# Linear attention and a two-matrix block on one Trainium2 core: Down stage in pairs of token groups, seven block products for eight in half the features

## The chip, the cores and the metric

The kernel runs on one core of one Trainium2 chip. The metric is the device time of one execution in microseconds (us), as the median of several runs. Beside the runs there is one profiled execution, whose trace gives the span from the first to the last instruction and every instruction's start and duration.

## The reference

```python
B, H, S, D = 4, 8, 768, 64          # batch, heads, sequence, head size; block = 64
for b in range(S // block):         # chunked linear attention with a decay per head
    qb, kb, vb = q[:, :, sl], k[:, :, sl], v[:, :, sl]
    intra = (qb kb^T * Dmask) vb
    inter = (qb * lam_pow) kv_state
    out[:, :, sl] = intra + inter
    kv_state = lam_block * kv_state + (kb * rev_pow)^T vb
x = out.transpose(0, 2, 1, 3).reshape(3072, 512)
h = x @ w_in                        # 512 x 2048
g = np.maximum(0.01 * h, h)
return g @ w_out                    # 2048 x 512
```

The data are float32; the two matrices arrive as float64 and are turned into float32 on the chip. A product of float32 matrices is made of three matmuls on reduced-precision parts (called h, l and m in the code), which have to be made of every operand first.

## The kernel before

**Tiling.** There are 24 chunks of 128 tokens, and four chunks make a group of T = 512 tokens; so NG = 6 groups. The 2048 features are cut into NP = 8 blocks p of 256.

**Stages.** A round (`round_of`) is the attention of one chunk: matmuls in `quad` (L313), VectorE and GpSimd steps for decay masks and states (L419, L423, L452, L459, L462), and the parts of x into the tiles X[g % 2] (L507 to L510). `up(g, p)` multiplies one group with one block of w_in (L640): per half block h and l passes, an ACT scaling in the bank (L658), the m pass, and the leaky ReLU on ACT (L661) into one of two buffers gs; a DMA (L664) stores 128 x 1024 values in memory, as G[g][p]. `to_float32` and `parts` turn float64 blocks of w_in and w_out into parts (L566 to L602); w_out goes to memory (`WO`) and comes back (`w_out_parts`, L621) when the last group of Up is done with the block's place in W. In the Down stage `down_load(g, p)` brings G[g][p] back (L675) into a ring of four slots and makes its parts: h on ACT (L682), l and m on VectorE (L683, L685). `down(g, p)` multiplies two blocks with w_out (L700): for each of four chunks of the group 12 matmuls, with the tokens as the stationary operand. Four pairs of banks hold the sums; after the eighth block ACT (L722) and VectorE (L729) combine a pair, and a DMA (L732) stores 128 x 512 results.

**Order.** Nothing is scheduled by the framework. Every step is handed to the class `Plan` with its engine, an assumed duration, and the names that it reads and writes. `Plan.emit` is a list scheduler: it gives each engine the step that can start first, ties by rank, and the program is issued in that order. A DMA's result is assumed 3.5 us after its end, and `slack` adds to that. Ranks come from the place in a list `seq`, which is written out by hand: rounds, `wi` (w_in), `up`, `wo`, `wp` (w_out's parts), `dl` and `dn`. All DMAs are issued on SyncE's queue (SP), in one order; an engine waits in its own order too, so a step that waits holds up what is behind it.

Of the kernel before, what the change touches and what calls it, by code (L numbers as in the profile page):

```python
# [8 lines left out]
F32 = mybir.dt.float32  # L9
F32R = mybir.dt.float32r  # L10
# [152 lines left out]
def kernel(  # L163
# [34 lines left out]

    DV = 10
# [21 lines left out]
    bank = {"b10": b1[0], "b11": b1[1], "b2": b2}  # L221
# [3 lines left out]
    raw = [sb([P, 2 * d_model], f"raw{i}") for i in range(NRAW)]  # L225
    lows = [sb([P, d_model], f"low{i}", I32) for i in range(2)]
    w32 = sb([P, 2, d_model], "w32")
    w32f = w32.rearrange("p h n -> p (h n)")
    tt = [raw[-1][:, i * T:(i + 1) * T] for i in range(2)]
    gs = [sb([P, 2, T], f"gs{i}") for i in range(2)]  # L230
    WO = [dram.tile([P, 2 * d_model], F32, name=f"wo{p}", tag=f"wo{p}") for p in range(NP)]
    G = [[dram.tile([P, 2 * T], F32, name=f"g{g}_{p}", tag=f"g{g}_{p}") for p in range(NP)] for g in range(NG)]
# [130 lines left out]
    def load_subs(c):  # L363
        b, n, i = of(c)
        count = run(c)[1]
        for nm, src, pieces in zip("kq", (k, q), subs(c, count)):
            for sub, lo, hi, keys in pieces:
                add("DVE", 0.0, lambda: None, [], keys)
                for y in range(lo, hi):
                    for a in range(4):  # L370
                        h = y // 2 + (2 * y + a // 2) % HP * 2
                        z = src[b, h, n * C:(n + count) * C, a % 2 * C4:(a % 2 + 1) * C4]
                        o = sub[a * C4:(a + 1) * C4, y - lo, :]
                        move(0.55, lambda o=o, z=z: nc.sync.dma_start(
                                out=o.rearrange("j (m i) -> j m i", i=C4), in_=z.rearrange("(m j) i -> j m i", j=C4)),
                            keys, [f"{nm}s{y}{a}"], issue=SUBL, rank=RUNS.get(c, (4.0, 0.4))[0] + RUNS.get(c, (4.0, 0.4))[1] * (4 * y + a))
# [179 lines left out]
    def to_float32(kind, p, h, dst, key, after=()):  # L556
# [20 lines left out]
        move(1.6, get, after, [f"raw{j}"])  # L577
# [9 lines left out]
    def parts(p, src, keys):  # L587
# [10 lines left out]
        difference(p)  # L598
# [12 lines left out]
    NR = 4  # L611
    graw = [att[:, j * 2 * T:(j + 1) * 2 * T] for j in range(NR)]

# [5 lines left out]
    def w_out_parts(p):  # L619
        j = p % NR  # L620
        add("DMA", 1.5, lambda: nc.sync.dma_start(out=graw[j], in_=WO[p]), [f"WO{p}"], [f"gr{j}"], rank=-3.0)  # L621
        parts(p, graw[j], [f"gr{j}"])


    n_t = n_g = 0
    n_b = -EARLY

    def up(g, p, lo=0, hi=GC):
# [20 lines left out]
        for fs in blocks:  # L649
# [9 lines left out]
            for i, f in enumerate(fs):  # L659
                add("PE", us, lambda f=f, d=b[:, i, :]: product(d, f, 2), keys("m"), [kb])  # L660
            add("ACT", ns, lambda b=b, r=r: nc.scalar.activation(out=r, in_=b, func=AF.Prelu, bias=0.0, scale=1.0 / WS, alpha=0.01),  # L661
                [kb], [f"gs{jg}"], rank=-1.5)
        move(1.5 * (hi - lo) / GC + 0.1,
            lambda: nc.sync.dma_start(out=G[g][p].rearrange("p (f t) -> p f t", f=2)[:, :, toks], in_=y), [f"gs{jg}"], [f"G{g}{p}"], slack=GSLACK)  # L664

    acc = [[z[:, i].rearrange("p y t -> p (y t)") for i in range(2)] for z in (psc, po)] + [
        [b1[0], b2], [b1[1], pt.rearrange("p y t -> p (y t)")]]
    ACC = [["psc", "psc"], ["po", "po"], ["b10", "b2"], ["b11", "pt"]]  # L670
    ring = [[X[j // 2][z].rearrange("p k t -> p (k t)")[:, j % 2 * 2 * T:(j % 2 + 1) * 2 * T] for z in range(3)] for j in range(NR)]

    def down_load(g, p):
        j = (g * NP + p) % NR
        add("DMA", 1.5, lambda: nc.sync.dma_start(out=graw[j], in_=G[g][p]), [f"G{g}{p}"], [f"gr{j}"])  # L675
        h, l, m = ring[j]
        reads = [f"gr{j}"]

        def wr(z):
            return [f"r{z}{j}"] + [f"x{z}{j // 2}{cc}" for cc in range(GC)] if g == 0 and p < NR else [f"r{z}{j}"]  # L680

        add("ACT", 1.05, lambda: nc.scalar.activation(out=h, in_=graw[j], func=AF.Copy, bias=0.0, scale=NEAR), reads, wr("h"))  # L682
        add("DVE", 1.25, lambda: nc.vector.scalar_tensor_tensor(l, graw[j], 1.0, h.bitcast(F32), op0=ALU.mult, op1=ALU.subtract),  # L683
            reads + [f"rh{j}"], wr("l"))
        add("DVE", 1.25, lambda: nc.vector.scalar_tensor_tensor(m, l.bitcast(F32), -S, h.bitcast(F32), op0=ALU.mult, op1=ALU.add),  # L685
            [f"rh{j}", f"rl{j}"], wr("m"))

    def down(g, p):

        nonlocal n_t  # L690
        for tb in range(GC):
            done = p + 2 == NP
            very_last = done and g == NG - 1 and tb == GC - 1

            def go(pps, zs, cols, tb=tb):
                for pp in pps:
                    j = (g * NP + pp) % NR
                    for f in range(2):
                        for z in zs:
                            nc.tensor.matmul(acc[tb][z // 2][:, cols], lhsT=ring[j][z][:, f * T + tb * P:f * T + (tb + 1) * P],  # L700
                                             rhs=W[pp][z][:, f * d_model:(f + 1) * d_model][:, cols],
                                             start=pp == 0 and f == 0 and z != 1, stop=pp == NP - 1 and f == 1,
                                             skip_group_check=True)

            def needs(pps, zs):
                return [f"{x}{z}{y}" for pp in pps for z in zs for x, y in (("r", (g * NP + pp) % NR), ("w", pp))]


            every = slice(0, d_model)
            halves = [slice(0, d_model // 2), slice(d_model // 2, d_model)]  # L710
            one, two = (p,), (p + 1,)
            order = [(one, (0, 1, 2), every), (two, (0, 1, 2), every)]
            if very_last:
                order = [(one + two, (0, 1), every)] + [(one + two, (2,), x) for x in halves]
            for pps, zs, cols in order:
                part_of = f"{halves.index(cols)}" if cols in halves else ""
                add("PE", 0.227 * 2 * len(pps) * len(zs) * (0.53 if part_of else 1.0), lambda pps=pps, zs=zs, cols=cols, go=go: go(pps, zs, cols),
                    needs(pps, ["hlm"[z] for z in zs]) + ([ACC[tb][1]] if part_of else []), sorted({ACC[tb][z // 2] + part_of for z in zs}))
            if done:
                jt, n_t = n_t % 2, n_t + 1  # L720
                t, y = tt[jt], gs[jt][:, 0, :]
                add("ACT", 0.6, lambda t=t, tb=tb: nc.scalar.activation(out=t, in_=acc[tb][0], func=AF.Copy, bias=0.0, scale=(1.0 + 1.0 / S) / U),  # L722
                    [ACC[tb][0]], [f"t{jt}"], rank=-1.5)
                rows = out[(g * GC + tb) * P:(g * GC + tb + 1) * P, :]
                n = 2 if very_last else 1
                for i in range(n):
                    cols = slice(i * d_model // n, (i + 1) * d_model // n)
                    add("DVE", 0.69 / n + 0.08 * (n - 1),
                        lambda t=t, y=y, tb=tb, cols=cols: nc.vector.scalar_tensor_tensor(  # L729
                            y[:, cols], acc[tb][1][:, cols], 1.0 / WS, t[:, cols], op0=ALU.mult, op1=ALU.add),  # L730
                        [f"t{jt}", ACC[tb][1]] + ([ACC[tb][1] + str(i)] if n == 2 else []), [f"gs{jt}{i}" if n == 2 else f"gs{jt}"], rank=-1.5)
                    add("DMA", 0.8 / n, lambda rows=rows, y=y, cols=cols: nc.sync.dma_start(out=rows[:, cols], in_=y[:, cols]),  # L732
                        [f"gs{jt}{i}" if n == 2 else f"gs{jt}"], [], rank=-1.5)

# [4 lines left out]
           ("up", 1, 4), ("r", 10), ("up", 1, 0), ("r", 11), ("up", 1, 6), ("up", 1, 5)]  # L742
    nxt, n_out, begin = 3 * GC, 0, len(seq)
    steps = [(g, p) for g in range(2, NG) for p in range(NP)]
    for n, (g, p) in enumerate(steps):
# [7 lines left out]
        if n_out < 2 * NP and n >= 1:  # L753
            seq.append(("wo", n_out // 2, n_out % 2, ["G%d%d" % steps[n - 1]]))
            n_out += 1
        if g == NG - 1:
            seq.append(("wp", p))
    for g in range(NG):
        for p in range(0, NP, 2):
            seq += [("dl", g, p), ("dl", g, p + 1), ("dn", g, p)]  # L760

    freed = False
    for n, x in enumerate(seq):
        plan.rank = float(n)
        steady = begin <= n and x[0] in ("r", "up", "wo")
# [13 lines left out]
        elif x[0] == "wp":  # L779
            if not freed:  # L780
                add("DVE", 0.0, lambda: None, [], ATT + [f"gr{j}" for j in range(NR)])
                add("ACT", 0.0, lambda: None, [], [f"raw{j}" for j in range(NRAW)] + ["t0", "t1"])
                freed = True
            w_out_parts(x[1])
        elif x[0] == "dl":
            plan.rank = n - 8.0
            down_load(*x[1:])
        else:
            down(*x[1:])
# [31 lines left out]
```

## Time and profile before

| | |
|---|---|
| median of 3 runs | 611.14 us (610.35 to 611.25) |
| profiled execution, span | 609.2 us (1.9 us below the median of the runs) |
| granted TensorE clock | 0.999 |
| TensorE matmul busy | 597.9 us, 98% of the span, 5386 matmuls |
| VectorE, ACT, GpSimd busy | 314.0, 269.0, 86.8 us |
| DMA | 105.18 MB, mean 173 GB/s; 123632 of 147754 packets under 512 B |
| Attention and Up / Down | 0 to about 347 us / about 347 to 606 us |

The profile gives busy time for each engine; a busy TensorE is not TensorE at its peak, since matmuls overlap: an instruction of 0.39 us starts every 0.227 us. The chain of waits, followed back from the last instruction, says which engine's work ended last at each moment. L640 is a line of the kernel before. DMA share is the mean busy share of the core's 16 DMA engines. Times to landing run from a DMA's issue to its completion.

### The profile page before, as it was taken

To read this page: it belongs to the slowest core of one execution; us is meant where nothing else is said; L and a number is where in the kernel's file an instruction comes from. 1 tells how busy PE (TensorE), PEld (TensorE's weight loads), DVE (VectorE), ACT (ScalarE), POOL (GpSimd) and SP (SyncE) were. 2 spreads that over 40 slices of the span, in tenths; PEclk is the share of its full clock that TensorE was granted. 3 is DMA by queue.
4 is the path that set the end of the run, shared out by engine and by line. 5 is a ranking of instruction groups with operands and counts; after the bars stand their busy time and mean duration, and the time that the engine had idled before them with its cause. 6 is when DMAs were issued, how large, how long until landed. Compare 5 with 4: busy or idle time off the path is not lost.

```text
span 609.2 us, 12932 instructions
## 1 busy us (share of the span) xinstructions
PE 597.9 (98%) x5386; PEld 495.6 (81%) x5386; DVE 314.0 (52%) x418; ACT 269.0 (44%) x430; POOL 86.8 (14%) x90
## 2 busy tenths in 40 slices
PE   7899999999999999999999999999999999999997
PEld 6687888888888878888788888888888888888886
DVE  5999764334243426326366745545454544635531
ACT  4688974444455646555577522222222313214111
POOL 1654412104133004104000000000000000000000
PEclk9999999999999999999999999999999999999999
DMA  9998774667888878886686843524333343333201
GB/s 213 232 272 245 221 203 124 173 133 199 199 213 238 212 227 214 216 244 210 233 300 217 290 145 103 173 69 139 138 104 131 112 138 105 138 104 122 86 1 69
DMA packets 147754, 105.18 MB, mean 173 GB/s; under 512 B 123632, under 2 KB 124400, under 8 KB 147696
## 3 DMA queue, kind: packets, MB, share of 16 engines
q1 hardware_dynamic: 147552, 104.36, 58.9%
q8 instruction: 42, 0.69, 0.5%
q14 instruction: 16, 0.13, 0.1%
q10 hardware_dynamic: 144, 0.00, 0.0%
HBM read 68.69 MB, written 35.65 MB: 171 GB/s over the span
## 4 chain that ended last, share of the span: by engine, by line
PE 92%; DVE 4%; DMA 2%; ACT 1%; issue 0%; POOL 0%; SPq 0%; DVEq 0%; ACTq 0%
PE b L640 40%; PE b L700 18%; PE po L700 11%; PE psc L700 11%; PE po L313 4%; PE pt L700 4%; PE psc L313 4%; DMA g<-gs 1%; DMA att<-in_v_dram 1%; DVE w L584 1%; DVE w L585 1%; DVE wm L602 1%; PE pt L403 1%; DMA att<-in_k_dram 1%; DVE wl L596 0%; DVE wh L593 0%
## 5 line engine op out<-in xcount | busy, mean ns | idle before, releaser
L682 ACT ACTIVATE xh<-att 128x1024 fp32r<-128x1024 f32 x48 | 50.7, 1060 | 148.7 <-PE b L700 140.7
L683 DVE SCALAR_TENSOR_TENSOR xl<-att,xh 128x1024 fp32r<-128x1024 f32 x48 | 58.6, 1223 | 98.6 <-ACT xh L682 98.6
L640 PE MATMUL b<-xm,wm 128*128 128x512 f32 (+2 forms) x392 | 104.5, 393 | 0.5 <-ACT b L658 0.5
L640 PE MATMUL b<-xl,wl 128*128 128x512 f32 (+2 forms) x392 | 103.4, 388 | 0.6 <-DVE wl L596 0.6
L640 PE MATMUL b<-xh,wh 128*128 128x512 f32 (+2 forms) x392 | 103.2, 387 | 0.8 <-ACT xh L507 0.8
L640 PEld LDWEIGHTS b<-xh,wh 128*128 128x128 f32 x392 | 73.0, 188 | 15.9 <-ACT xh L507 0.9
L640 PEld LDWEIGHTS b<-xl,wl 128*128 128x128 f32 x392 | 72.8, 188 | 15.6 <-DVE wl L596 1.0
L640 PEld LDWEIGHTS b<-xm,wm 128*128 128x128 f32 x392 | 71.5, 188 | 15.7 <-ACT b L658 0.9
L658 ACT ACTIVATE b<-b 128x512 f32<-128x512 f32 (+2 forms) x97 | 56.1, 580 | 60.3 <-PE b L640 60.1
L661 ACT ACTIVATE gs<-b 128x512 f32<-128x512 f32 (+2 forms) x97 | 56.8, 591 | 44.9 <-PE b L640 38.8
L700 PE MATMUL b<-wl,xl 128*128 128x512 f32 x192 | 74.8, 390 | 0.0
L700 PE MATMUL b<-wh,xh 128*128 128x512 f32 x192 | 74.8, 390 | 0.0
L685 DVE SCALAR_TENSOR_TENSOR xm<-xl,xh 128x1024 fp32r<-128x1024 f32 x48 | 58.7, 1226 | 4.7
L462 POOL TENSOR_TENSOR att<-att 128x256 f32<-128x256 f32 x40 | 35.0, 876 | 57.2 <-DVE att L459 55.9
L700 PEld LDWEIGHTS b<-wl,xl 128*128 128x128 f32 x192 | 36.1, 188 | 7.4
L700 PEld LDWEIGHTS b<-wh,xh 128*128 128x128 f32 x192 | 36.0, 188 | 7.5
L423 POOL TENSOR_TENSOR att<-att 128x512 f32<-128x512 f32 (+1 forms) x20 | 24.2, 1211 | 96.2 <-DVE att L383 47.4
L452 DVE TENSOR_TENSOR att<-psc,att 128x512 f32<-128x512 f32 x24 | 16.5, 690 | 41.0 <-PE psc L313 41.0
L584 DVE TENSOR_SCALAR w<-w 128x512 int32<-128x512 int32 x32 | 19.2, 599 | 35.4 <-ACT w L578 35.3
L700 PE MATMUL po<-wm,xm 128*128 128x512 f32 x96 | 37.4, 390 | 0.0
L700 PE MATMUL po<-wh,xh 128*128 128x512 f32 x96 | 37.4, 390 | 0.0
L700 PE MATMUL po<-wl,xl 128*128 128x512 f32 x96 | 37.4, 390 | 0.0
(73 smaller groups left out, 805.4 us busy)
## 6 DMA issues: line engine op xcount, KB each, us to landing
att<-g SPq DMA_DIRECT2D x48, 512.0 KB, 3.3
g<-gs SPq DMA_DIRECT2D x47, 512.0 KB, 4.0
raw<-in_moe_w_in_dram SPq DMA_DIRECT2D x16, 512.0 KB, 5.4
raw<-in_moe_w_out_dram SPq DMA_DIRECT2D x16, 512.0 KB, 4.7
att<-in_k_dram SPq DMA_DIRECT2D x48, 128.0 KB, 4.2
att<-in_v_dram SPq DMA_DIRECT2D x24, 256.0 KB, 4.4
out_dram<-gs SPq DMA_DIRECT2D x23, 256.0 KB, 2.1
wo<-w SPq DMA_DIRECT2D x8, 512.0 KB, 5.9
```

What stands on the lines that cost most here:

```text
L313: nc.tensor.matmul(dst[HALF[cols]], lhsT=lhsT[HALF[rows]], rhs=rhs[HALF[rows]], start=start, stop=True, skip_group_check=True)
L423: add(eng, us, lambda: e.tensor_tensor(o, x, _bc(pow_q, 2, 2)[:, :, m, :], op=ALU.mult), ["fq", dep], [f"qsT{i}"])
L452: add("DVE", 0.69, lambda: nc.vector.tensor_tensor(sc, psc[:, :, lower, :], decay, op=ALU.mult), ["psc", "fk"], ["sc"])
L462: add("POOL", 0.7, lambda new=new, j=j: nc.gpsimd.tensor_tensor(state[(j + 1) % 4], new, _bc(lam_c, 2, D), op=ALU.mult), [f"st{j % 4}", "f ...
L584: add("DVE", 0.42, lambda: nc.vector.tensor_scalar(d, d, 3, None, op0=ALU.logical_shift_left), [], [key])
L640: nc.tensor.matmul(dst, lhsT=w[z][:, kk * 2 * P + f * P:kk * 2 * P + (f + 1) * P], rhs=x[z][:, kk, toks], start=start and kk == 0, stop=kk ...
L658: add("ACT", ns, lambda b=b: nc.scalar.activation(out=b, in_=b, func=AF.Copy, bias=0.0, scale=S + 1.0), [], [kb], rank=-1.5)
L661: add("ACT", ns, lambda b=b, r=r: nc.scalar.activation(out=r, in_=b, func=AF.Prelu, bias=0.0, scale=1.0 / WS, alpha=0.01), [kb], [f"gs{jg} ...
L682: add("ACT", 1.05, lambda: nc.scalar.activation(out=h, in_=graw[j], func=AF.Copy, bias=0.0, scale=NEAR), reads, wr("h"))
L683: add("DVE", 1.25, lambda: nc.vector.scalar_tensor_tensor(l, graw[j], 1.0, h.bitcast(F32), op0=ALU.mult, op1=ALU.subtract), reads + [f"rh{ ...
L685: add("DVE", 1.25, lambda: nc.vector.scalar_tensor_tensor(m, l.bitcast(F32), -S, h.bitcast(F32), op0=ALU.mult, op1=ALU.add), [f"rh{j}", f" ...
L700: nc.tensor.matmul(acc[tb][z // 2][:, cols], lhsT=ring[j][z][:, f * T + tb * P:f * T + (tb + 1) * P], rhs=W[pp][z][:, f * d_model:(f + 1) ...
```

## The change

The change rewrites the Down stage. Groups are taken in pairs (0 and 1, 2 and 3, 4 and 5). For the blocks p below `NS` = 4, the two groups and the two halves (f) of each block make a 2 x 2 matrix of activation blocks, and w_out's two halves of features and two halves of its columns another; their product is made with seven block products and additions (Strassen's method in Winograd's form) in place of eight. The blocks 4 to 7 keep plain products.

What is new or moves:

- Up: for p < 4 one half of each block is negated by VectorE (`flip`) before it is stored, and the stores go to arrays `BB[g][p // 2]`, each holding two blocks.
- `copies_of`: three DRAM to DRAM copies of 512 KB on SP per pair and per two blocks, 18 in all. `gather`: four accumulating DMAs of 512 KB on GpSimd's queue per pair and two blocks, 24 in all; each adds one activation block to another in memory. They form the sums of activations.
- `w_out_parts` for p < 4: VectorE forms the sums of w_out's quarters in `staging`, then parts of four quarters go to W[p] and parts of three quarters to the places of the attention's tiles and of `lows`. The m part is now a subtraction on VectorE and a scaling on ACT (`minus`).
- `unit` takes the place of `down_load`: the DMA loads into the slot's m part, which is later overwritten. The ring has five slots.
- `strassen(pr, t, u)`: 12 matmuls; `plain(pr, p, gi)`: 24. The stationary operand is now w_out and the tokens move (512), so that results stand transposed in the banks X, Z, Y and V. `copy_banks` and `add_banks` carry sums from bank to bank (ACT, VectorE).
- `leave`: VectorE transposes a bank in blocks of 32, and four DMAs per bank store it in pieces of 32 values; two staging buffers take turns.
- `seq` is written anew from the last Up group on, and the first half of w_out's block 0 is taken one step earlier.

```diff
+    NS = 4
+    LEAD = 8.0
+    WSLACK = 0.75
+    ADDS = 6.0
...
+            for i, f in enumerate(fs if p < NS else [None]):
+                ...
+                flip = f is not None and f == g % 2
...
+                if flip:
+                    add("DVE", 0.15 + 0.25 * n / T, lambda o=o: nc.vector.tensor_scalar(o, o, -1.0, None, op0=ALU.mult), [], [f"gs{jg}"], rank=-1.5)
...
+    def unit(src, keys):
...
+        add("DMA", 1.5, go, keys, wr("m"))
+        add("ACT", 1.05, head, [f"rm{j}"], wr("h"))
+        add("DVE", 1.25, low, [f"rm{j}", f"rh{j}"], wr("l"))
+        add("DVE", 1.25, middle, [f"rh{j}", f"rl{j}"], [f"rm{j}"])
+        return j
...
+    def copies_of(pr, u):
+        g = 2 * pr
+        for i, (z, f) in enumerate(((T1, 0), (T2, 0), (T4, 1))):
+            move(1.5, lambda z=z, f=f: nc.sync.dma_start(out=z[pr][u], in_=BK[g][f][u]), [f"B{g}{p}{f}" for p in (2 * u, 2 * u + 1)],
+                [f"T{(1, 2, 4)[i]}{g}{p}" for p in (2 * u, 2 * u + 1)])
...
+        for z, kz, x, kx in ((T1[pr], keys("T1", g), BK[g + 1][0], keys("B", g + 1, 0)), (BK[g + 1][0], keys("B", g + 1, 0), BK[g + 1][1], keys("B", g + 1, 1)),
+                             (T2[pr], keys("T2", g), BK[g + 1][0], keys("B", g + 1, 0)), (T4[pr], keys("T4", g), T2[pr], keys("T2", g))):
+            plan.slack = ADDS
+            add("POOL", 1.2, lambda z=z, x=x: nc.gpsimd.dma_start(out=z[u], in_=x[u], accum_op=ALU.add, max_dma_last_dim=4 * 2 * T), kx, kz, rank=-8.0)
+            plan.slack = 0.0
...
+    KINDS = {1: (0, "X"), 5: (1, "V"), 6: (-1, "Z"), 2: (2, "X"), 7: (-2, "Z"), 3: (-3, "Y"), 4: (3, "Z")}
...
+        w, d = KINDS[t]
+
+        def go():
+            for i, p in enumerate(ps_):
+                for c in range(2):
+                    product(acc[d][c], j, i * T, lambda z, p=p, c=c: operand(z, p, w)[:, c * P:(c + 1) * P],
+                            first=t in (1, 5) and u == 0 and i == 0)
...
+        y = gs[0][:, o, lo:lo + n]
+        add("DVE", 0.1 + 0.6 * n / T, lambda: nc.vector.transpose(out=y, in_=b[:, lo:lo + n]), [kb, k], [f"o{o}"] + (["gs0"] if n_o <= 2 else []), rank=-1.5)
+
+        def store():
+            for a in range(4):
+                nc.sync.dma_start(out=out[g * T + lo:g * T + lo + n, c * P + a * C4:c * P + (a + 1) * C4].rearrange("(b i) j -> i b j", i=C4),
+                                  in_=y[a * C4:(a + 1) * C4, :].rearrange("i (b j) -> i b j", j=C4))
...
+        late = [n(p, 1, pr - 1) for p in range(NS, NP)] if pr else []
+        if pr:
+            seq += [late[0], s(1, 0), late[1], s(1, 1), ("copy", "Z", "X"), late[2], s(6, 0), late[3], s(6, 1), ("copy", "Y", "Z"),
+                    s(5, 0), s(5, 1), ("add", "Y", "V"), s(7, 0), s(7, 1), ("add", "V", "Z"),
+                    s(3, 0), n(4, 0), s(2, 0), n(5, 0), s(3, 1), s(2, 1), n(6, 0), s(4, 0), s(4, 1), n(7, 0)]
+        else:
+            i = seq.index(("up", NG - 1, NP - 1))
+            seq[i:i] = [s(1, 0)]
+            seq += [s(1, 1), ("copy", "Z", "X"), s(6, 0), s(6, 1), ("copy", "Y", "Z"), s(5, 0), s(5, 1), ("add", "Y", "V"), ("wp", 4), s(7, 0), s(7, 1), ("add", "V", "Z"), ("wp", 5),
+                    s(3, 0), n(4, 0), s(2, 0), ("wp", 6), n(5, 0), s(3, 1), s(2, 1), ("wp", 7), n(6, 0), s(4, 0), s(4, 1), n(7, 0)]
+    seq += [n(p, 1) for p in range(NS, NP)]
```

The two steps of a group are s(t, u), product t of the two blocks 2u and 2u + 1, and n(p, gi), the plain block p of group gi of the pair.

## The prediction

> **What bounds the kernel now.** I read the page first (busy shares, granted clock, chain), then the windows by stage, the groups by form, the timeline of the last microseconds, and the DMA answers.
>
> ```profile
> PE 597.9 (98%) x5386; PEld 495.6 (81%) x5386; DVE 314.0 (52%) x418; ACT 269.0 (44%) x430; POOL 86.8 (14%) x90
> ...
> PE 92%; DVE 4%; DMA 2%; ACT 1%; issue 0%; POOL 0%; SPq 0%; DVEq 0%; ACTq 0%
> PE b L640 40%; PE b L700 18%; PE po L700 11%; PE psc L700 11%; PE po L313 4%; PE pt L700 4%; PE psc L313 4%; DMA g<-gs 1%; DMA att<-in_v_dram 1%; DVE w L584 1%; DVE w L585 1%; DVE wm L602 1%; PE pt L403 1%; DMA att<-in_k_dram 1%; DVE wl L596 0%; DVE wh L593 0%
> ```
>
> TensorE is the bound: 92% of the chain, of which L700 (Down) has 44% and L640 (Up) 40%. So only matmuls removed, or waits put between matmuls, can move the end. By stage (columns: length, then busy time and count of each engine, clock, DMA share, GB/s):
>
> ```profile
> 180.00:240.00 60.00, 59.52 (x703) 49.03 (x702) 26.25 (x47) 32.81 (x58) 13.74 (x15) 1.00 0.85 229
> 240.00:300.00 60.00, 59.72 (x778) 49.31 (x778) 23.55 (x44) 35.02 (x62) 11.78 (x13) 1.00 0.75 219
> 300.00:347.00 47.00, 47.00 (x209) 38.91 (x208) 29.79 (x31) 31.53 (x50) 0.00 (x0) 1.00 0.77 266
> 400.00:500.00 100.00, 100.00 (x442) 82.83 (x442) 50.41 (x47) 23.68 (x26) 0.00 (x0) 1.00 0.36 121
> ```
>
> Down (400:500) has a full TensorE at clock 1.00, VectorE half idle, DMA at 0.36. Attention and Up have a TensorE just as full, but DMA engines already at 0.75 to 0.85: the change puts new transfers there.
>
> **The matmuls.** The chain in order of time has rows like this:
>
> ```profile
> 347.17 2.72 PE po L700 x12
> ```
>
> So one 128x128x512 matmul costs 2.72/12 = 0.2267 us. Down has 48 (group, block) pairs of 24, so 1152. After, for each of three pairs of groups: blocks 0 to 3 take 14 units of 12, 168 where 192 stood; blocks 4 to 7 keep 192. That is 1080, and two matmuls that only open the Z banks. 70 x 0.2267 = 15.9 us less; the last bank in halves (12 at 0.139, from 1.11 us for 8 at the end) gives 0.1 back: **-15.8 us**, all on the path.
>
> **Feeding the units (first pair).** A unit needs a load, one ACT pass and two VectorE passes:
>
> ```profile
> L685 DVE SCALAR_TENSOR_TENSOR xm<-xl,xh 128x1024 fp32r<-128x1024 f32 x48 | 58.7, 1226 | 4.7
> L683 DVE SCALAR_TENSOR_TENSOR xl<-att,xh 128x1024 fp32r<-128x1024 f32 x48 | 58.6, 1223 | 98.6 <-ACT xh L682 98.6
> L682 ACT ACTIVATE xh<-att 128x1024 fp32r<-128x1024 f32 x48 | 50.7, 1060 | 148.7 <-PE b L700 140.7 <-issue 8.0
> ...
> att<-g SPq DMA_DIRECT2D x48, 512.0 KB, 3.3
> ```
>
> VectorE gives 2.45 us to a unit. Before, a unit fed 24 matmuls (5.44 us); now 42 of 66 units feed 12 (2.72 us). From a slot's release to its next use: issue 0.3, landing 3.3, ACT 1.06, VectorE 2.45, so 7.1 us. I walked the orders of the changed program with these rows, time 0 at the first matmul of product 6 (s60; "s" is product and half, "n" a plain block). s50 loads into the slot that s11 leaves at -0.9, so its passes end at 6.3 where its third matmul wants the middle part at 5.9: 0.4. VectorE then makes s51 (8.8), s71 (11.2) and only then s70 (12.5, 13.7), which TensorE wants at 11.8: 2.0. Later the passes of n4, s20, n5, s31, s21 and four bank additions (0.69 each, as L452's 0.69) run on without a gap up to the weights of block 5, done at 33.6, with ACT's scaling 34.7; n5 wants them at 32.9: 1.9. **+4.3 us**; bounds 1 (loads earlier) and 8 (each landing at 4.5, as att<-wo does). In pairs two and three the late blocks of the pair before lie between the units; the same walk leaves every unit 1.3 us or more ahead: 0.
>
> The weight work added to the last Up group: per block 0 to 3, four 256-wide tensor operations (0.41 as L459), 0.27, 0.69 (L593), 1.22 + 1.22, and twice 0.95 for the three-quarter matrices: 6.9 us, 28 for four; with blocks 4 and 6 (6.3), four units (9.8) and sign flips (2) 46 us of VectorE beside 50 us of TensorE (group five with s10 and s11 in it). TensorE covers it; if a late one uncovers, it is in the bound of 8.
>
> **The end.** Before, the last matmul is followed by 3.6 us:
>
> ```profile
> 605.22 0.40 PE L700 MATMUL pt<-wm,xm 128*128 128x256 f32 x2
> 605.71 0.76 DVE L729 SCALAR_TENSOR_TENSOR gs<-pt,raw 128x256 f32<-128x256 f32 x2 [1.72 <-PE pt L700]
> 606.16 0.81 SPq L732 DMA_DIRECT2D out_dram<-gs  x2
> ```
>
> After, each bank leaves by a VectorE transpose (0.69, as L383's 128x512 at 0.68) and four stores of 128 B pieces. SP's rate for such pieces:
>
> ```profile
> 101.17 3.80 SPq L374 DMA_DIRECT2D raw<-in_k_dram  x7
> 107.99 2.49 SPq L374 DMA_DIRECT2D w<-in_q_dram  x5
> ```
>
> 0.5 us each, so 2.0 us a bank, while the last banks finish every 1.36 us; and the two staging halves make each transpose wait for the stores of the bank two before. With E the last matmul's end: V0 ends at E-4.4, transposed by -3.6, issued to -1.6, landed at 0.0 (2.1 us, out_dram<-gs); Y0's transpose waits for that, ends 0.75, issued to 2.75, landed 4.35; the last half bank's transpose waits for that, 4.8, issued to 6.8, landed 8.4. So 8.5 against 3.6: +4.9; with SP at 0.34 (large transfers) +3.5. I take **+4.5 us**; up to 7 if such pieces are slower as writes (no row shows one). SP spends 2 us on each of the other 20 banks too, but unit loads behind them come out in time in the walk.
>
> **Attention and Up.** TensorE's work is the same. ACT's count per bank is the same. VectorE gets 24 flips of 128x512 at 0.43 to 0.6 (L584), 10 to 14 us under an engine about half idle; they hold a store back by that and whatever stands before them on VectorE. On SP a copy waits for the landing of the store that it reads; behind it stand the loads of k and v and the next stores. SP gets 18 copies of 512 KB, POOL 24 sums of 512 KB, of which 16 and 12 copies fall in about 105 to 285 us (by the stores that they follow). One 512 KB transfer keeps the 16 engines busy 1.55 us (121 GB/s at a share of 0.36). No row shows a sum: between 1.55 and twice that, since it reads both operands. So 12 x 1.55 + 16 x 1.55 to 3.1 = 43 to 68 us, into 39 us that the shares leave free (180 less 0.75 x 75 + 0.85 x 60 + 0.75 x 45). But slices in these windows reach 390 GB/s at the same share, so that much of "busy" is waiting in small packets; transfers will be late, most have a round in hand (POOL and VectorE wait for them, TensorE hardly: 0.8 us idle from 180 to 300). I take **+2.5 us**, bounds -1 (the planner lays the order anew) and +10.
>
> POOL's queue: a sum waits on POOL for the sum before it, and behind it stand the attention steps (state scaling L462, 0.88 us, and q scaling L423). The plan leaves 7.3 us per sum. Nearest rows: 3.3 (att<-g) to 5.9 (wo<-w) from issue to landing; I take 6 to 8, so nothing. The Trainium skill, "DMA: Bandwidth & Descriptors", Anatomy of one DMA, gives 2.0 us plus bytes / 436 GB/s for a transfer issued by GpSimd, by which a sum would land in 3.2 us (an estimate) and POOL would never be held; no row here shows it.
>
> **Sum.** 609.2 - 15.8 + 4.3 + 4.5 + 2.5 = 604.7 of span. The median of the runs is 1.9 us above the profiled span: **606.6 us**.
>
> **Rivals.**
> Everything covered (0.17): first pair 1, end 3.5, Up 0: 597.9 + 1.9 = 599.8. For it: VectorE at 50% in Down; against it: the walk.
> Slower: DMA engines become the bound from 105 to 285 us (0.22). For it: 68 us of new transfers against 39 free, and stores whose landing frees gs. The point is 7 us: if more than 7 of the possible 29 us reach TensorE, the gain is gone. Half of it, 14.5 in place of 2.5: 618.6. Against it: TensorE idle of 0.8 us beside a share of 0.85.
> POOL held by its sums (0.08): 12 sums wait for an earlier one; a round is 9.5 us (the chain has rounds from 227.8, 237.3, 246.8) and its chain of states needs 2 x (0.41 + 0.88) + 1.75 of matmuls, so TensorE waits from about 7.3 + 5 on: at 13.3 us a sum, 12 x 1 = 12 more, 618.6.
> The 128 B stores are slow (0.08): at three times the landing (6.3) the two landings in the last chain and the last itself add 12.6: 619. The Trainium skill, same page, Specifications, has 512 B as the least size for line rate, with a read-modify-write below it, a rule against this change; no run so far shows a small write.
> That the work isn't less is no rival: the order has 70 matmuls fewer.
>
> **Numbers.** Forecast as summed: 0.45. 8 in 10: from 599.5 (all covered) to 619 (the slower cases at their prices). Of the forecast and the covered case nearly all lies below 609.9, some of it spills over; the other three lie mostly above 612.4. What a measurement tells from no change is 0.2%, 1.2 us: faster 0.64, same 0.06, slower 0.30.
>
> **What would show it.** Right: Down's matmuls 1080 long at 0.2267; gaps of TensorE only between the first pair's s50 and n5, some 4 us, released by VectorE; 8 us from the last matmul to the end, SP at 0.5 us per store. Wrong: TensorE idle between 105 and 285 us behind POOL or DMA (landing of g<-gs and of in_k well above 4.2 us); sums longer than 12 us; gaps in the second or third pair; no gap at all.

## The result: 10% slower

The changed kernel takes 675.3 us (median of 4 runs, 672.6 to 678.1) where the kernel before takes 611.0: a ratio of 1.1045, 95% interval 1.1008 to 1.1082. The forecast was 606.6, the range 599.5 to 619.0. The profiled execution has a span of 671.9 us, 62.7 us more than before's 609.2.

The page of the changed kernel, its lines of busy time and chain, then its slices of TensorE, granted clock and DMA:

```profile
PE 607.1 (90%) x5318; PEld 495.3 (74%) x5318; DVE 389.4 (58%) x524; ACT 296.7 (44%) x460; POOL 103.0 (15%) x114
...
PE   8899999996787997849799997899999999999994
...
PEclk9999999997987999888899998899999999999998
DMA  9989878799989989997885699653757346583433
...
PE 42%; DMA 6%; DVE 2%; SPq 2%; ACT 1%; issue 1%; DVEq 0%; ACTq 0%
```

TensorE has 68 matmul records fewer and is busy 9.2 us longer. At full clock the matmuls that are left would keep it busy 597.9 - 15.8 = 582.1 us; so 25.0 us are longer matmuls. The granted clock of the whole execution is 0.957, before 0.999, which fits them. Idle time went from 11.3 to 64.8 us. The weak slices lie in the first two thirds, nearly all of them under a full row of DMA; Down is full behind its first slices. By stage, in columns as before:

```profile
180.00:240.00 60.00, 48.42 (x531) 38.98 (x530) 24.02 (x46) 29.20 (x51) 12.12 (x13) 0.89 0.95 267
240.00:300.00 60.00, 47.72 (x533) 38.65 (x531) 19.70 (x37) 24.09 (x42) 15.92 (x20) 0.92 0.99 234
300.00:360.00 60.00, 53.40 (x613) 43.03 (x613) 25.68 (x47) 31.20 (x57) 8.76 (x9) 0.91 0.77 233
520.00:620.00 100.00, 97.70 (x429) 79.90 (x428) 76.76 (x71) 35.15 (x39) 0.00 (x0) 1.00 0.56 160
```

From 180 to 300 us the kernel before ran 1481 matmuls (large ones and the small ones of attention together); here 1064 are run, at a clock of 0.89 to 0.92, with the DMA engines at 0.95 to 0.99 (before 0.85 and 0.75).

One stall shows how a full DMA reaches TensorE. From the timeline of the changed kernel (start, length, engine, instruction, and in brackets the idle time before it with what ended it); the two rows below them are from the timeline of TensorE alone:

```profile
292.27 0.41 SPq L580 DMA_DIRECT2D raws<-in_moe_w_out_dram  x1
292.49 1.07 PE L702 MATMUL b<-xl,wl 128*128 128x512 f32 x4
299.74 0.66 ACT L589 ACTIVATE w<-raws 128x512 f32<-128x512 f32 x1 [9.11 <-DMA raws<-in_moe_w_out_dram]
301.55 1.59 ACT L720 ACTIVATE b<-b 128x512 f32<-128x512 f32 x3
```

```profile
302.22 5.23 PE L702 MATMUL b<-xm,wm 128*128 128x512 f32 x12 [8.67 <-ACT b L720]
307.29 1.07 PE L702 MATMUL b<-xh,wh 128*128 128x512 f32 x4
```

A load of w_out is issued at 292.27 and lands about 7.4 us later. ACT, which takes its steps in order, stands before L589 for 9.11 us. Behind L589 stand three scalings of banks (L720) that have nothing to do with the load; all three of TensorE's banks wait for them, and TensorE stands for 8.67 us. Then its next 12 matmuls take from 302.22 to 307.29, 5.07 us where 12 took 2.72 in the chain of before: the granted clock of this stretch is 0.53, and 1.00 behind it. So the stall costs 8.67 + 2.35 us. The Trainium skill, "TensorE: Matmul & The Clock Gate", HAM oscillation, says just that: a gap longer than about 3.4 us puts the clock back to half, and every DMA wait in a loop pays it again. The trace agrees here, but the length does not decide it in these runs: a gap of 2.33 us at 282.18, behind the small matmuls of attention, was followed by half rate too (four matmuls took 1.70 us, from 284.00 to 285.70, in place of 0.91), while one of 2.83 us in run b1 (experiment 4), at 296.80, left the clock at 1.00.

The chain goes through further such places in the last third of Up (start, length, what):

```profile
320.99 8.46 DMA raws<-in_moe_w_out_dram
...
345.13 8.09 DMA raws<-t
```

Between 100 and 380 us nine gaps of TensorE are over 1 us, 37.3 us together. Five of them, 23.8 us, end with ACT's work on banks, each time behind a wait of ACT for a load of w_out; one more, 3.50 us, ends with VectorE, which had waited for ACT in the same way. But the second longest gap is another path: attention itself waits for a load. The profile names no releaser for it ("issue"), but a load of v that was issued at 143.79 landed 14.9 us later, at 158.7, just ahead of the row, and in b1 the two longest gaps, 6.52 and 4.53 us, are named as waits for v. A row on this DMA, then TensorE's in the timeline:

```profile
att<-in_v_dram SPq DMA_DIRECT2D x1, 256.0 KB, 14.9
158.80 1.98 PE L324 MATMUL psc<-att 64*64 64x64 f32 x64 [6.57 <-issue]
```

### The profile page after: what moved, and what is told of

The parts are those of the page before. It is cut to its first block, busy times and chain, and to the rows that moved or that the text cites. A ratio compares the mean times of both kernels' runs of the same rounds, so it can differ in the third digit from the quotient of the medians.

```text
span 671.9 us, 13196 instructions
## 1 busy us (share of the span) xinstructions
PE 607.1 (90%) x5318; PEld 495.3 (74%) x5318; DVE 389.4 (58%) x524; ACT 296.7 (44%) x460; POOL 103.0 (15%) x114
## 4 chain that ended last, share of the span: by engine, by line
PE 42%; DMA 6%; DVE 2%; SPq 2%; ACT 1%; issue 1%; DVEq 0%; ACTq 0%
PE b L702 11%; PE psc L806 10%; PE po L806 10%; PE b L806 9%; PE pt L806 3%; SPq L872 2%; DMA xm<-t 1%; DMA xm<-g 1%; DMA raws<-in_moe_w_out_dram 1%; DMA raws<-t 1%; DVE xl L773 1%; DVE xm L777 1%; ACT xh L769 1%; DMA xm<-b 1%; DMA out_dram<-gs 1%
## 5 line engine op out<-in xcount | busy, mean ns | idle before, releaser
L702 PE MATMUL b<-xm,wm 128*128 128x512 f32 (+2 forms) x392 | 110.8, 413 | 16.6 <-ACT b L720 16.5
L769 ACT ACTIVATE xh<-xm 128x1024 fp32r<-128x1024 f32 x53 | 56.2, 1063 | 102.7 <-DMA xm<-t 35.4
L773 DVE SCALAR_TENSOR_TENSOR xl<-xm,xh 128x1024 fp32r<-128x1024 f32 x53 | 64.6, 1220 | 41.4 <-ACT xh L769 41.2
L720 ACT ACTIVATE b<-b 128x512 f32<-128x512 f32 (+2 forms) x97 | 55.7, 581 | 45.5 <-PE b L702 45.1
L324 PE MATMUL po<-att 64*64 64x64 f32 x1472 | 33.4, 223 | 7.2 <-DVE att L502 3.8
L324 PEld LDWEIGHTS po<-att 64*64 64x64 f32 x1472 | 27.4, 135 | 15.9 <-issue 6.1
L430 POOL TENSOR_TENSOR att<-att 128x512 f32<-128x512 f32 (+1 forms) x23 | 25.8, 1120 | 82.5 <-DMA att<-in_k_dram 55.3
L324 PE MATMUL psc<-att 64*64 64x64 f32 x1472 | 29.3, 227 | 9.9 <-issue 6.6
L434 POOL TENSOR_TENSOR att<-att 128x512 f32<-128x512 f32 (+1 forms) x20 | 26.2, 1308 | 75.7 <-DVE att L394 46.4
L589 ACT ACTIVATE w<-raws 128x512 f32<-128x512 f32 x32 | 21.0, 665 | 36.7 <-DMA raws<-in_moe_w_out_dram 28.3
L324 PEld LDWEIGHTS psc<-att 64*64 64x64 f32 x1472 | 26.7, 142 | 11.5 <-issue 8.3
L806 PE MATMUL psc<-xm,wm 128*128 128x512 f32 x84 | 32.9, 392 | 1.5 <-DVE xm L777 1.5
```

What stands on the lines that cost most here:

```text
L324: nc.tensor.matmul(dst[HALF[cols]], lhsT=lhsT[HALF[rows]], rhs=rhs[HALF[rows]], start=start, stop=True, skip_group_check=True)
L430: lambda e="POOL": ENG[e].tensor_tensor(kr[nr], kr[nr], _bc(pow_k, 3, D)[nr], op=ALU.mult), ["fk"], [f"k{i}"])
L434: add(eng, us, lambda: e.tensor_tensor(o, x, _bc(pow_q, 2, 2)[:, :, m, :], op=ALU.mult), ["fq", dep], [f"qsT{i}"])
L589: add("ACT", 0.67, lambda: nc.scalar.activation(out=dst, in_=words(1, F32), func=AF.Abs, scale=2.0 ** -110), [f"raw{j}"], [key])
L702: nc.tensor.matmul(dst, lhsT=w[z][:, kk * 2 * P + f * P:kk * 2 * P + (f + 1) * P], rhs=x[z][:, kk, toks], start=start and kk == 0, stop=kk ...
L720: add("ACT", ns, lambda b=b: nc.scalar.activation(out=b, in_=b, func=AF.Copy, bias=0.0, scale=S + 1.0), [], [kb], rank=-1.5)
```

## The experiments

Three accounts of the loss were set against each other: E (or T), the engine time that the 42 added transfers take from the 16 DMA engines while attention and Up need them; Q, the queues: sums and copies that wait on GpSimd and SyncE hold up what is behind them; P, the planner's order: the change also sets the slack for w_out loads from 4.0 to 0.75 us (`WSLACK`), so that ACT's conversions come ahead of scalings. Ratios are to runs of the kernel before on the same chip; a number in brackets is the 95% interval. "Engine time" below is the DMA share of the whole span times the span, good to some 4 us in differences, since shares have two digits.

**1. Taking the transfers away, in the same order.**

```diff
-            move(1.5, lambda z=z, f=f: nc.sync.dma_start(out=z[pr][u], in_=BK[g][f][u]), ...
+            move(1.5, lambda: None, ...
-            add("POOL", 1.2, lambda z=z, x=x: nc.gpsimd.dma_start(out=z[u], in_=x[u], accum_op=ALU.add, ...), ...
+            add("POOL", 1.2, lambda: None, ...
```

> The changed kernel in the order that its planner made, without the 18 copies and the 24 sums; products 4 to 7 read activation blocks that are not summed. Theory T (transfers: the 42 added transfers fill the DMA engines between 105 and 345 us, so that loads and stores which attention and Up wait for come late): nearly the whole 69 us lost ahead of Down come back, 604 to 612 us, the stalls of TensorE ahead of 345 us vanish, and in_k lands in 3 us again. Theory P (order: the planner now expects a w_out load 3.25 us earlier and puts ACT's conversions ahead of the scalings of banks, which then wait): the order is the same here, so a good part of the loss stays, 630 to 665 us, with ACT's waits for raws<-w_out as long as they were.

621.6 us, 1.0162 (1.013 to 1.0194). Of the 64 us, 53.7 came back. The idle time of TensorE fell by 34.4 us (64.8 to 30.4) and its busy time by 17.5 (607.1 to 589.6). It missed both expectations: better than P's, but 10.9 us above the kernel before where T expected none; that rest is taken up in 5.

**2. Copies without sums** (the second edit alone).

> The changed kernel without the 24 sums; the 18 copies stay. Leaves out the sums, so the products read the copies. Theory T, by DMA engine time: 18 copies at 1.55 us are 28 us of the 65 to 102 us of all 42; with 39 us free of them the engines are just not full, so 608 to 620 us. Theory Q (queue of GpSimd: sums wait there for their operands, 57.5 us for stores of gs alone, and hold up the state scalings behind them): no sum, no hold, 606 to 612 us. Theory P: 630 to 665 us.

635.0 us, 1.0397 (1.0355 to 1.044): the 18 copies cost 13.4 us over a1. Q had expected the queue of GpSimd to be the cost and 612 us at most; T's 608 to 620 was also too low. Engine time: 409 us in a1, 438 here, so 1.6 us a copy.

**3. Plain transfers in place of sums.**

```diff
-nc.gpsimd.dma_start(out=z[u], in_=x[u], accum_op=ALU.add, max_dma_last_dim=4 * 2 * T)
+nc.gpsimd.dma_start(out=z[u], in_=x[u])
```

> The changed kernel with the 24 accumulating transfers turned into plain transfers of the same blocks on the same queue with the same waits; leaves out the additions. Theory T, by bytes read and written: a sum reads its destination too, so a third of its bytes go; 24 x 0.8 us of engine time less, 650 to 665 us. If the accumulation itself is what is slow: 610 to 640 us. Theory Q (the waits on GpSimd's queue): the waits are the same, 665 to 676 us.

658.4 us, 1.0774 (1.0718 to 1.0831), in T's range, though T had only 19 us of engine time go and the shares give 38. So the 24 transfers cost 23.4 us as plain ones and 16.9 more as sums; their engine time is 41 us plain and 79 us as sums (479 and 517 less 438), 1.7 and 3.3 us each. The loss follows the engine time: 13.4 for 29, 23.4 for 41, 40.4 for 79 us.

**4. The traffic alone, and its size.** The kernel before with the 18 copies and 24 sums at the same places, into arrays that nothing reads; then the same with an eighth of the columns, all waits kept:

```diff
+            move(1.5, lambda z=z, p=p: nc.sync.dma_start(out=z[pr][u], in_=G[g][p]), ...)
+            add("POOL", 1.2, lambda z=z, x=x: nc.gpsimd.dma_start(out=z, in_=x, accum_op=ALU.add, ...), ...)
```
```diff
-out=z[pr][u], in_=G[g][p]
+out=z[pr][u][:, :P], in_=G[g][p][:, :P]
-out=z, in_=x, accum_op
+out=z[:, :P], in_=x[:, :P], accum_op
```

> The kernel before with the traffic of the change alone: 18 copies of 512 KB on SP and 24 accumulating transfers on GpSimd's queue at the same places of the order, into arrays that nothing reads. Result unchanged. Theory T (the transfers by themselves cost what the change without them, 621.6 us, lacks to 675.3): 611 + 54, so 655 to 670 us. Rival T2 (they cost so much only beside what else the change puts there, sign flips, earlier w_out loads, fuller SyncE queue): 620 to 640 us. By the prediction's own term: 613.5 us.

> The kernel before with the same 18 copies and 24 accumulating transfers at the same places, with the same waits on SyncE's and GpSimd's queues, but of 128 columns in place of 1024: 64 KB each. Result unchanged. Theory E (the time of the DMA engines: 98 us of it by the shares with and without the transfers): an eighth of the 50 us of the full transfers is left, 614 to 620 us. Theory Q (the queues: copies wait on SyncE for stores to land with loads of k, q and v behind them, sums wait on GpSimd for copies and stores with state scalings behind them): waits for stores and for landings stay, 630 to 655 us.

661.5 us, 1.0812 (1.0774 to 1.0851), and 614.7 us, 1.0063 (1.0042 to 1.0083); T and E had both. The transfers alone, in a kernel without any other part of the change, cost 50.3 us; with an eighth of the bytes 3.7 us. Their number, places and waits are the same in both, and so are the durations that the planner assumes, so the queues and a new order account for 3.7 us at most: the rest is the bytes. E holds, Q falls. The window of b1 that answers to before's from 240 to 300 us:

```profile
240.00:300.00 60.00, 47.11 (x524) 37.26 (x524) 19.00 (x32) 24.63 (x45) 15.78 (x19) 0.91 0.94 225
```

Nearly the same DMA share, clock and idle TensorE as in the changed kernel (0.94, 0.91 and 12.9 us; there 0.99, 0.92 and 12.3). In b1 the loss is 29.7 us of idle time and 19.5 of longer matmuls.

**5. The planner's slack.** 4.0 in the changed kernel, 4.0 in a1, and 0.75 in the kernel before:

```diff
-    WSLACK = 0.75
+    WSLACK = 4.0
```

> The changed kernel with the planner's slack for w_out loads back at 4.0 us (0.75 in the change). Theory P: the conversions go behind the scalings of banks, ACT no longer waits 7.5, 5.8 and 8.5 us for raws<-w_out with scalings behind it, 625 to 650 us. Theory T: the stalls go elsewhere since the DMA engines stay full, 665 to 678 us.

> The changed kernel without copies and sums (products 4 to 7 read activation blocks that are not summed) and with the slack for w_out loads back at 4.0 us. Theory P2: the two stalls of 2.9 and 3.4 us behind ACT's waits for raws vanish and no stall comes in their place while the DMA engines have room, 606 to 612 us. If the later conversions then hold up the parts of w_out at the start of Down, as with the transfers (685.9 us against 675.3 us): 620 to 635 us.

> The kernel before with the planner's slack for w_out loads at 0.75 us in place of 4.0, which the change sets. Result unchanged. Theory P2 (what the change loses without its transfers, some 17 us more than forecast, is ACT waiting for w_out loads ahead of scalings): 618 to 628 us. Otherwise 611 to 614 us.

685.9 us, 1.1235 (1.1183 to 1.1287); 633.1 us, 1.0357 (1.0335 to 1.038); 616.4 us, 1.0085 (1.007 to 1.01). The slack has a price of 5.3 us in the kernel before, through two stalls of 2.4 and 1.4 us behind ACT and the slow matmuls after them. But putting it back makes the changed kernel slower, with or without transfers. In a5 no gap of TensorE between 60 and 340 us is over 1.8 us, where a1 has 2.94 and 3.36; then w_out's preparation comes too late, TensorE stands twice in product 1, 7.04 us the first time, and product 6 starts at 379.7 (a1: 362.5). This is the chain of a5 ahead of it, in order of time:

```profile
352.61 6.43 DMA w<-wo
361.11 0.70 DVE wh L604
361.84 1.23 DVE wl L607
363.09 1.23 DVE wm L615
```

So P is a real, smaller cost: the change needs w_out's quarters prepared before Down, one block after another through one staging buffer, and pays for it either as ACT's waits in Up or at the start of Down. It can explain a part of a1's rest, not the 53.7 us.

**6. The transfers in Down.** Copies and sums of pairs two and three behind s11 of the pair before, six copies in a row:

```diff
...
+        i = seq.index(("s", pr - 1, 1, 1)) + 1
+        seq[i:i] = [("cp", pr, 0, m), ("cp", pr, 1, m), ("ga", pr, 0), ("ga", pr, 1)]
```

> The changed kernel with the copies and sums of pairs two and three moved into Down, each while the pair before is multiplied; those of the first pair stay. Result unchanged. Theory T (the place decides: DMA engines at 0.75 to 0.95 in Up, at 0.56 to 0.61 in Down): a third of the 54 us is left in Up and nothing is lost in Down, 635 to 645 us. Rival (28 transfers in 160 us of Down make the unit loads late, since a unit has one landing in hand): 650 to 675 us, with gaps of TensorE in pairs one and two.

685.1 us, 1.1214 (1.116 to 1.1268): the rival's outcome, and worse. TensorE stood in Down for 18.2, 6.1, 11.3 and 9.4 us. SyncE's rows and ACT's wait show the first:

```profile
371.79 1.18 SPq L788 DMA_DIRECT2D t<-b  x2
...
376.88 2.62 SPq L788 DMA_DIRECT2D t<-b  x4
379.61 3.20 SPq L765 DMA_DIRECT2D xm<-t  x2
```

```profile
398.86 1.06 ACT L769 ACTIVATE xh<-xm 128x1024 fp32r<-128x1024 f32 x1 [15.04 <-DMA xm<-t]
```

The unit's load issued behind these six copies, at 379.61, landed 19.2 us later; behind the second six it was 17.5 us. A burst is a delay for whatever comes next.

**7. A kernel made for the transfers.** The first pair multiplied plainly (its Up then needs no transfer), order and slack of the kernel before, copies behind single steps of Down, w_out's quarters prepared a second time there, four staging halves at the end. 48 matmuls fewer than before:

```diff
-            for i, f in enumerate(fs if p < NS else [None]):
+            for i, f in enumerate(fs if p < NS and g > 1 else [None]):
...
+            for p in range(NS):
+                seq += [n(p, 0), n(p, 1), ("wq", p)]
...
+                seq[j:j] = [("cp", r, u, i, "mn%d%d%d" % x[1:])] + ([("ga", r, u)] if i == 2 else [])
```

> The change for pairs two and three only, with all its added transfers moved out of attention and Up: the first pair is multiplied plainly with the kernel before's order ahead of it (slack 4.0, no sign flips for groups 0 and 1); the copies of pairs two and three are issued one by one behind steps of the first pair's Down, where a unit feeds 24 matmuls; w_out's parts for blocks 0 to 3 are made a second time there; four staging halves at the end, half the last stores on ACT's queue. Result unchanged. 48 matmuls fewer than before: -10.9 us. Theory E (what costs is the DMA engines' time in attention and Up): Up ends at 347 us as before, some 3 us lost at the start of Down and 3 at the end, 602 to 612 us. Theory B (the transfers cost about half their engine time wherever they stand, 65 us here): 630 to 645 us.

> As d1_last_two (plain first pair, transfers of pairs two and three in Down), but one copy per step: pair two's behind the first six steps of Down, pair three's behind six later ones up to the middle of pair two; half of all result stores on ACT's queue; slack of the sums 3.0 us. Result unchanged. In d1 TensorE stood for 11 us in two bursts, at 373 us behind four copies in a row and at 447 to 476 us, and ran 9 us slower around them. Theory E' (the bytes cost only where they come in a burst that a unit load must queue behind): most of these 20 us come back, 607 to 614 us, as fast as the kernel before. Theory B (every added transfer costs about half its engine time wherever it stands): 620 to 632 us.

> d2_spread in the same order without its 12 copies and 16 sums; products 4 to 7 of pairs two and three read activation blocks that are not summed. In d2 TensorE stood and ran slow for some 20 us between 378 and 480 us, where two things meet: the transfers, and w_out's second preparation on VectorE with four loads. If the transfers are the cause: the stalls vanish, 603 to 608 us (10.9 us of matmuls less, 3 us lost at the end, 1 to 4 at the start of Down). If the second preparation is: the stalls stay, 616 to 621 us.

d1: 626.0 us, 1.0273 (1.0223 to 1.0324), between the ranges of both theories. d2, its copies spread out: 620.6 us, 1.0149 (1.0111 to 1.0187). e1, d2 without the transfers: 607.9 us, 0.9941 (0.9923 to 0.996). Up is undisturbed in d1 and d2 (no gap over 1.2 and 1.9 us from 60 to 340 us). Spreading brought 5 us, not most of 20. By its time d2 lies in theory B's range, but not by its price: the transfers cost 12.7 us of the 67 us of engine time that they take in d2 (478 less 411): a fifth, where in attention and Up it was half (53.7 of 108, 50.3 of 95), and half is what B says. e1 is in the range given for the transfers as the cause: the second preparation costs little. With its sums for nothing, this form for two pairs is worth 0.6%; no kernel here that computes the sums beat the one before.

**8. One transfer at a time.** In the quiet Down of the kernel before, four copies on SyncE, each followed on GpSimd's queue by a sum (two of them) or by a plain copy (two):

```diff
+            add("POOL", 1.2, lambda: nc.gpsimd.dma_start(out=T1[g], in_=G[0][1], accum_op=ALU.add, ...), ...)
+            add("POOL", 1.2, lambda: nc.gpsimd.dma_start(out=T2[g], in_=T1[g]), ...)
```

> The kernel before with four single transfers of 512 KB on SyncE's queue in the quiet part of Down (DMA engines at 0.36), each followed on GpSimd's queue by a second one: for groups 1 and 2 an accumulating transfer, for groups 3 and 4 a plain copy. Result unchanged, time 611 to 613 us. It measures the landing without a queue: by the prediction 6 to 8 us for a sum. Theory S (a sum is slow by itself): 7 us or more here too, and a plain copy 4 to 5. Theory L (only the load makes it 8 to 9 us): both 4 to 5 us.

610.9 us (one run, no cost that can be told). The rows on DMAs, of this kernel (median us to landing at the end) and of the changed one:

```profile
t<-g SPq DMA_DIRECT2D x4, 512.0 KB, 4.5
t<-g POOLq DMA_DIRECT2D x2, 512.0 KB, 5.2
t<-t POOLq DMA_DIRECT2D x2, 512.0 KB, 3.8
```

```profile
t<-b SPq DMA_DIRECT2D x18, 512.0 KB, 8.1
t<-b POOLq DMA_DIRECT2D x12, 512.0 KB, 8.7
```

By itself a sum lands in 5.2 us, 1.4 later than a plain copy on the same queue (two of each); in the changed kernel the groups of sums and copies take 7.8 to 9.1 us: the load makes most of it (theory L, the sum a little above its 4 to 5). The fit of the Trainium skill, "DMA: Bandwidth & Descriptors", Anatomy of one DMA, gave 3.2 us (an estimate); the plain copy comes near it, the sum does not.

## Why the prediction was wrong

TensorE's time line, cut at the start of product 6 (s60) and at the last matmul, puts the terms beside what they measured. Before, Down's 261.2 us of matmuls end at 605.6, so Down starts in effect at 344.4; with s10, s11 and the two opening matmuls ahead of it, s60 would start at 350.3 if nothing were lost. In the changed kernel it starts at 407.2, in a1 at 362.5. From s60 to the last matmul there are 239.5 us of matmuls.

| term | forecast | without transfers (a1) | changed kernel |
|---|---|---|---|
| matmuls | -15.8 | -15.8 | -15.8 |
| attention and Up, to s60 | +2.5 | +12.2 | +56.9 |
| feeding, s60 to the last matmul | +4.3 | +8.7 | +16.1 |
| end | +4.5 | +5.7 | +5.5 |
| sum of the span | -4.5 | +10.8 | +62.7 |

**Matmuls: right.** The chain in order of time has the same row as before, and the count went down as forecast:

```profile
444.47 2.72 PE psc L806 x12
```

**Attention and Up: the step that failed.** The prediction had the size of the added load about right: 43 to 68 us for the 28 transfers ahead of 285 us, and 108 us were measured for all 42, a sum just above its bounds (3.3 us where they were 1.55 to 3.1). It had the 39 us that were free. What failed was the overlap: "most have a round in hand ... TensorE hardly", with +2.5 us and a bound of +10, where 53.7 (a1) and 50.3 us (b1) were measured for the transfers. Its reason, that much of a busy DMA is waiting and so room, did not hold: from 240 to 300 us the share rose from 0.75 to 0.99, but what was moved only from 219 to 234 GB/s. A TensorE that idles 0.8 us beside a share of 0.85 can also mean that the order fits the landings of that kernel, not that there is room; this reading fits the runs, but no run tests it by itself. In the changed kernel a late load held ACT's queue, ACT's queue held all three banks, or a late load held attention directly, and each of the seven stops of TensorE from 2.33 to 8.67 us between 100 us and s60 was followed by a lower clock. The rival "DMA engines become the bound" named the mechanism, but capped it at 68 - 39 = 29 us and took half: 14.5. The cap assumed that the free time could be used and that a microsecond of stall costs one. The 18 copies of a2 alone, 29 us of engine time and so less than the 39 free, cost 13.4 us; and 25.0 of the 62.7 us are slow matmuls.

**A line of the change that was not costed.** `WSLACK` changes the planner's order by itself: 5.3 us in the kernel before (b2). Of a1's 12.2 us ahead of s60, two stalls of 2.94 and 3.36 us stand behind ACT's waits for w_out, and the 12 matmuls behind each, slower by 2.0 and 1.7 us, bring it to 10.0.

**Feeding: right in kind, beside a new wait.** The forecast had 0.4 us at s50, 2.0 at s70 and 1.9 at n5, with VectorE's passes as the limit. Without the transfers (a1) these three gaps are there, in the places and behind the passes that the walk has, 0.83, 2.15 (1.39 and 0.76 in the part behind it) and 1.28 us, 4.3 together:

```profile
369.52 0.50 PE L806 MATMUL b<-xm,wm 128*128 128x512 f32 x1 [0.83 <-DVE xm L777]
376.44 0.50 PE L806 MATMUL po<-xl,att 128*128 128x512 f32 x1 [1.39 <-DVE xl L773]
398.36 0.50 PE L806 MATMUL psc<-xm,wm 128*128 128x512 f32 x1 [1.28 <-ACT wm L617]
```

In the changed kernel TensorE's rows are:

```profile
416.91 0.80 PE L806 MATMUL b<-xh,wh 128*128 128x512 f32 x1 [3.96 <-ACT xh L769]
...
428.19 0.49 PE L806 MATMUL po<-xl,att 128*128 128x512 f32 x1 [1.53 <-DVE xl L773]
429.45 0.50 PE L806 MATMUL po<-xm,att 128*128 128x512 f32 x1 [0.77 <-DVE xm L777]
```

s70 lost 2.3 us, as walked. n5 lost none. s50 lost 5.0 (3.96 and the two parts behind it, 0.47 and 0.54): its load of the sum T1 took 9.80 us to land behind the last sums. The walk had that landing at 3.3, the quiet figure. In the later pairs, where the walk had 1.3 us in hand, one unit of pair two was late by 1.6 us and one of pair three by 0.7. These gaps are 9.6 of the 16.1 us; most of the rest is the low clock behind s50 and s70 (0.84 from s60 to 440 us), as in the first row, 0.80 for a matmul of 0.39.

**End: right in kind, 1 us short.** 9.1 us from the last matmul, forecast 8.5. The chain is the one that was walked, staging halves waiting for stores at 0.51 us each:

```profile
665.18 0.45 DVE L868 STREAM_TRANSPOSE gs<-b 128x256 f32<-128x256 f32 x1 [1.59 <-DMA out_dram<-gs]
667.20 0.45 DVE L868 STREAM_TRANSPOSE gs<-b 128x256 f32<-128x256 f32 x1 [1.57 <-DMA out_dram<-gs]
```

**The other rivals.** POOL held by its sums: no; the 24 sums landed in 6.0 to 9.9 us each, under the 12.3 (7.3 + 5) from which it would make TensorE wait, GpSimd is named for none of the long gaps, and b3 keeps the waits for 3.7 us. Slow 128 B stores: no; 64 KB of them land in 1.9 us, where that rival had 6.3. The rule that speaks against them (the Trainium skill, "DMA: Bandwidth & Descriptors", Specifications: at least 512 B for line rate) shows no price here, where SyncE's 0.51 us per store is the limit.

What stays open: how the last 2 us of a1's 12.2 ahead of s60 divide between the sign flips, the fuller ACT and the order; whether the DMA engines or the memory behind them set the longer landings, since every run that adds to one adds to the other; and what an order planned for landings of 8 us would lose.

## What to carry to other kernels

A DMA share of 0.75 to 0.85 under a full TensorE was not 0.15 to 0.25 of room. In this kernel added transfers cost half their engine time in attention and Up (0.50 and 0.53), and a fifth one at a time in Down (d2); moved to Down in bursts of six (c1) they made the kernel slower still. Ask of every late load which engine's queue waits for it and what unrelated work stands behind that wait, and add the slow clock after each longer stop of TensorE. A removal of 6% of one stage's matmuls has to be paid for in the stage that has room, and read every constant of a scheduler in a diff as an edit of its own.

## What the runs showed of the hardware

- A sum in memory (accumulating DMA of 512 KB) keeps the DMA engines busy for about 3.3 us, a plain copy for 1.6 to 1.7; alone they land in 5.2 and 3.8 us on GpSimd's queue.
- Behind six copies of 512 KB in a row the next load of 512 KB on the queue landed after 19.2 and 17.5 us (c1).
- In the changed kernel each gap of TensorE of 2.33 to 8.67 us between 100 us and s60, and the one of 3.96 us at s50, was followed by matmuls at or near half rate. In other runs gaps of 2.36 (b2) and 2.43 us (b1) were too, and gaps of 2.50 (a4) and 2.83 us (b1) were not. Longer matmuls made 25.0 us over the changed kernel, and 19.5 over the kernel before with the transfers (b1).
- The last stores on two queues (d1) took SyncE 7.96 and ACT 5.94 us for ten each, so 20 in 8 us against 10.3 on SyncE alone. With four staging halves in place of two as well, the end fell from 9.1 to 6.8 us, not by half.
